# The second MLP layer of 256-token chunks as a seven-product block product, with its sums on GpSimd

## The chip, the cores and the metric

The kernel runs on one core of a Trainium2 chip. The metric is device microseconds (us) of one execution. A core has five engines, each of which executes its own queue of instructions in the order of the program: TensorE (PE in the profile; PEld is its loading of stationary operands), VectorE (DVE), ScalarE (ACT), GpSimd (POOL) and SyncE (SP, which here issues all the DMAs). They wait for one another on semaphores.

## The reference, cut to what matters

```python
# q, k, v: (8, 8, 576, 64) float32; w_in: (512, 2048), w_out: (2048, 512)
scores = scale * q @ k.T                       # 64 heads of 576 x 576
kth    = 32nd largest of each row
attn   = softmax of the row, with all below kth masked out
x      = (attn @ v)  laid out as 4608 tokens x 512
h      = x @ w_in
g      = max(0.01 * h, h)
out    = g @ w_out                             # 4608 x 512
```

The weights come as 64-bit floats; the kernel turns them to float32 itself, at the start.

## The kernel before, in words

**Attention.** Work is cut into 144 units, 18 for each of the 8 batches. A unit is 128 rows of queries for one pair of heads: two score matrices of 128 x 576. Of the 18, 16 are 128 query rows of one pair ("whole"), and 2 are the 64 left-over rows of two pairs ("left"). A unit goes through these stages:

- `scores`: q·k on PE into PSUM (L235), for two units at a time, and four copies by ACT into `s_sb` (L242).
- `top_k` on DVE: one pairwise max and min of the halves of each row (L306, two instructions), then four rounds of MAX8 (L311) and MATCH_REPLACE8 (L314). The 32nd value ends up in `tops`.
- `limits` on POOL: three tiny instructions (L324, L325, L326) that make `nleast` and `nbias` of `tops`.
- `mask` (L330) and `exponents` (L333) on ACT, two of each, and `sums` (L338), which makes `ze`.
- `reciprocals` on DVE (L342: `rz` of `ze`), and `normalize` on POOL (L345, two instructions of 128 x 576).
- `transpose`: two copies by ACT that split the 32-bit weights into 16-bit halves (L354), two DMAs to DRAM (L355), and one transposing DMA back to `wT` (L359).
- `values`: `wT` times v on PE (L398, L410), for two units at a time, and copies by ACT to `x` (L422).

**The MLP.** The tokens are taken in 19 chunks, two of 128 and 17 of 256. For a chunk of 256, the first layer makes 8 pieces `ph` (two blocks of 128 of the 2048 hidden columns each, L467: matmuls with 256 moving columns, four deep), and ACT writes each through leaky ReLU to `gT` (L473). The second layer then makes, for each 128 tokens, one `pz` of 512 columns, 16 matmuls deep (L479), which ACT copies to `o_sb` (L488), and SP sends out (L489). A float32 matmul shows as two MATMUL records in the profile, each with its LDWEIGHTS.

**The order** is written out by hand. The main loop runs over steps s, one unit each. In step s, DVE does `top_k` of unit s. Within the step these go to the queues in this order: `limits(s-1)` and `normalize(s-2)` early, then on ACT `mask(s-1)`, the first of `exponents(s-1)`, the two splits of s-2, the second of `exponents(s-1)`, `sums(s-1)`. At the end of each even step come `values` of two units (s-4 and s-3 from unit 14 on), their copies to `x`, and the `scores` of units s+2 and s+3 with their four copies. Between these parts there are seven places a step (`mlp_steps`), at which the MLP generator of the running chunk is advanced piece by piece; the budget of a place is the work of the chunk divided by the places left until the next chunk's tokens are ready. The last place of a step lies after the scores. What a piece gives to ACT, POOL and SP stands in their queues at the same place.

The rows of chunk 17 are ready 8 units before the end, those of chunk 18 with the last unit; what is left is done after the last step.

**Scores kept in DRAM.** For the 12 units 26, 27, 34, 35, 62, 63, 70, 71, 98, 99, 106, 107, the scores are made in the first steps (`keep_scores`, L286 on PE, L290 on ACT), stored in DRAM and fetched when due (`fetch_scores`); `load_early` brings their q and k into buffers named `raw`, three of which hold the raw weights at the start. Later those buffers serve as three more pairs of q and k buffers, besides five.

The second layer as it stands in the code:

```python
for r0 in range(0, n, P):
    pz = ps_ml.tile([P, 512], F32, name="pz", tag="ml")
    for f in range(NFC):
        nc.tensor.matmul(pz[0:m, 0:DMODEL], gT[:, f, r0:r0 + m], w_out[f // 4][:, f % 4, :], ...)
```

Of the kernel before, what the change touches and what calls it, by code (L numbers as in the profile page):

```python
# [20 lines left out]
def kernel(  # L21
# [23 lines left out]
    HP = DMODEL // P  # L45
# [20 lines left out]
    kept = ctx.enter_context(tc.tile_pool(name="kept", bufs=1, space=bass.MemoryType.DRAM))  # L66
# [93 lines left out]
    qk_of, v_of = {}, {}  # L160

    def load_qk(pi, at_once=True):
        if pi % (LOADED + 3) < LOADED:
            qt = loads.tile([P, S], F32, name="qt")
            kt = loads.tile([P, S], F32, name="kt")
        else:
            raw = raws.tile([P, WCH, 4], U16, name="raw").rearrange("p n w -> p (n w)").bitcast(F32)
            qt, kt = raw[:, 0:S], raw[:, S:2 * S]
# [75 lines left out]
    def first_scores(u):  # L244
# [10 lines left out]
        u.s = [u.both[:, i, :] for i in range(2)]  # L255
        for i in range(2):
            nc.scalar.copy(u.s[i].rearrange("p (h n) -> p h n", h=2), ps[i][:, :, 0:HS])  # L257

    early_of = {}

    def load_early(us):

        raw = raws.tile([P, WCH, 4], U16, name="raw").rearrange("p n w -> p (n w)").bitcast(F32)
        at = 0
        for pi in sorted({u.pairs[0] for u in us}):
            kt = raw[:, at:at + S]
            nc.sync.dma_start(kt, kT[pi])
            at += S
            for u in us:
                if u.pairs[0] == pi:  # L270
                    early_of[u] = raw[:, at:at + P], kt
                    nc.sync.dma_start(early_of[u][0], qT[pi][:, u.q0:u.q0 + P])
                    at += P

    kept_of = {}

    def keep_scores(u):

        k = len(kept_of)
        qt, kt = early_of.pop(u)  # L280
        ps = [ps_sc.tile([P, 2, 512], F32, name="wide", bufs=2) if (2 * k + i) % 3 else
              ps_sc.tile([P, 2, 512], F32, name="narrow") for i in range(2)]
        for half in range(2):
            for i, _, side, _ in u.parts:
                d = slice(side * D, (side + 1) * D)
                nc.tensor.matmul(ps[i][:, half, 0:HS], qt[d, :], kt[d, half * HS:(half + 1) * HS],  # L286
                                 start=True, stop=True)
        both = gT.rearrange("p f n -> p (f n)")[:, k % 3 * 2 * S:(k % 3 + 1) * 2 * S]
        for i in range(2):
            nc.scalar.copy(both[:, i * S:(i + 1) * S].rearrange("p (h n) -> p h n", h=2), ps[i][:, :, 0:HS])  # L290
        kept_of[u] = kept.tile([P, 2 * S], F32, name=f"kept{k}")
        nc.sync.dma_start(kept_of[u], both)

    def fetch_scores(u):
        u.both = work.tile([P, 2, S], F32, name="s_sb", bufs=5)
        u.s = [u.both[:, i, :] for i in range(2)]
        nc.sync.dma_start(u.both.rearrange("p i n -> p (i n)"), kept_of[u])

    def top_k(u):

# [147 lines left out]
    def turned(j, g_of):  # L448
# [3 lines left out]
        nc.scalar.copy(gT[:, 4 * j:4 * (j + 1), 0:P], pt)  # L452
        yield 2 * P

    def mlp(ch):

        n = CHUNKS[ch]
        t0 = sum(CHUNKS[:ch])
        x = x_of[ch]
        if ch < EARLY:  # L460
            yield from hidden_of_few(ch, x)
        for f0 in range(0, NFC if ch >= EARLY else 0, 2):
            ph = ps_ml.tile([P, 2, CHMAX], F32, name="ph", tag="ml")
            for i in range(2):
                f = f0 + i
                for c in range(HP):
                    nc.tensor.matmul(  # L467
                        ph[:, i, 0:n], w_in[c][:, f * P:(f + 1) * P], x[c][:, 0:n],
                        start=(c == 0), stop=(c == HP - 1),
                    )  # L470
                    if c == 1 or i == 0 and c == HP - 1:
                        yield 2 * max(n, 225)
            nc.scalar.activation(gT[:, f0:f0 + 2, 0:n], ph[:, :, 0:n], AF.Prelu, alpha=SLOPE)  # L473
            yield 2 * max(n, 225)
        for r0 in range(0, n, P):
            m = min(P, n - r0)
            pz = ps_ml.tile([P, 512], F32, name="pz", tag="ml")
            for f in range(NFC):
                nc.tensor.matmul(  # L479
                    pz[0:m, 0:DMODEL], gT[:, f, r0:r0 + m], w_out[f // 4][:, f % 4, :],  # L480
                    start=(f == 0), stop=(f == NFC - 1),
                )
# [4 lines left out]
            o_sb = work.tile([P, DMODEL], F32, name="o_sb", bufs=1)  # L487
            nc.scalar.copy(o_sb[0:m], pz[0:m, 0:DMODEL])  # L488
            nc.sync.dma_start(out[t0 + r0:t0 + r0 + m, :], o_sb[0:m])  # L489
# [40 lines left out]

    steps = units

    KEPT = (26, 62, 98)
    EARLY_SCORES = {0: 4, 1: 2, 2: 1, 3: 2, 4: 1, 5: 2}

    def unit(n):
        return steps[n] if 0 <= n < len(steps) else None

# [25 lines left out]
    with tc.manual_schedule():  # L564
        last = {p: n for n, u in enumerate(steps) for p in u.pairs}
        starts = {p: n for n, u in reversed(list(enumerate(steps))) for p in u.pairs}

        to_keep = [[steps[n] for n in (a, a + 1, a + 8, a + 9)] for a in KEPT]
        early_units = {u for us in to_keep for u in us}
        to_load, to_keep = list(to_keep), [u for us in to_keep for u in us]  # L570
        assert all(len(u.pairs) == 1 for u in to_keep)

        def score_early(count):

            for _ in range(min(count, len(to_keep))):
                keep_scores(to_keep.pop(0))
                if len(to_keep) % 4 == 0 and to_load:
                    load_early(to_load.pop(0))

        def load_more(s):  # L580

            at_once = 2
# [13 lines left out]
                    break  # L596
            while len(qk_of) < NPAIR:
                n = len(qk_of)
                if n < LOADED or not to_keep and n < LOADED + 3:
                    load_qk(n)  # L600
                elif not to_keep and last[n - LOADED - 3] + 8 <= s and not waiting:
                    load_qk(n, at_once=False)
                else:
                    break

# [4 lines left out]
        for n in range(len(jobs) + 1):  # L610
# [11 lines left out]
                    pass  # L622
            if n:
                load_weights(n + 2)
            if n >= len(jobs) - 2 and to_load:
                load_early(to_load.pop(0))
            if 0 <= n - len(jobs) + HP + 1 < HP:
                load_qk(n - len(jobs) + HP + 1)

# [18 lines left out]
        def keep(weighed, *place):  # L648
            for u, po in weighed:
                keep_values(u.pairs[0], po, u.b, u.q0)  # L650
            attended(*place)

        for s in range(len(steps) + LAG + 1):
            assert s < 7 or not to_keep
            cur, old, older, new = unit(s), unit(s - 1), unit(s - 2), ()
            if s % 2 == 0:
                new = [u for u in steps[s + 2:s + 4] if u]
# [33 lines left out]
                keep_transposed(older) if s - 2 in HASTY else transpose(older, lambda: mlp_steps(budget))  # L691
            if not older or s - 2 in HASTY:
                mlp_steps(budget)
            if unit(s + 3) in early_units:
                fetch_scores(unit(s + 3))
            else:
                load_waiting()
            slot()
            slot()
            mlp_steps(budget)  # L700
# [3 lines left out]
            mlp_steps(budget)  # L704
            if not at_once:
                keep(weighed, s, MIDDLE)
            if new and new[0] in early_units:
                new = ()
# [69 lines left out]
```

## Time and profile before

| what | value |
|---|---|
| median of 3 runs | 1460.23 us (1459.14 to 1461.59) |
| the profiled execution's own time | 1464.25 us |
| its span, first to last instruction | 1462.5 us |
| PE busy | 1399.0 us, 96% of the span |
| DVE busy | 1313.9 us, 90% |
| ACT busy | 1103.2 us, 75% |
| POOL busy | 738.5 us, 50% |
| mean granted clock of PE | 0.986 |
| first and last start of `top_k` (L306) | 61.32 us, 1366.41 us |

A row of a group reads: line, engine, operation, output<-input, shapes, how many; then busy time of the group in us, mean of one in ns; then the idle time of the engine just before these instructions, and what ended it. Matmuls are pipelined, so that busy time divided by the number of records is nearer to the cost of one than its mean duration is: 482.6 us / 2176 = 222 ns for a record with 256 moving columns (L467), 505.7 us / 1152 = 439 ns for one with 512 (L479).

### The profile page before, as it was taken

To read this page: it belongs to the slowest core of one execution; us is meant where nothing else is said; L and a number is where in the kernel's file an instruction comes from. 1 tells how busy PE (TensorE), PEld (TensorE's weight loads), DVE (VectorE), ACT (ScalarE), POOL (GpSimd) and SP (SyncE) were. 2 spreads that over 40 slices of the span, in tenths; PEclk is the share of its full clock that TensorE was granted. 3 is DMA by queue.
4 is the path that set the end of the run, shared out by engine and by line. 5 is a ranking of instruction groups with operands and counts; after the bars stand their busy time and mean duration, and the time that the engine had idled before them with its cause. 6 is when DMAs were issued, how large, how long until landed. Compare 5 with 4: busy or idle time off the path is not lost.

```text
span 1462.5 us, 25892 instructions
## 1 busy us (share of the span) xinstructions
PE 1399.0 (96%) x8980; PEld 904.8 (62%) x8980; DVE 1313.9 (90%) x3401; ACT 1103.2 (75%) x1984; POOL 738.5 (50%) x744
## 2 busy tenths in 40 slices
PE   7847989999999999999999999999999999999998
PEld 2324547575666666666666666666666666666674
DVE  7998999999999999999999999999999999999500
ACT  8878877777787787777787878778778787778710
POOL 3245555555555555555555555555555555555500
PEclk9968999999999999999999999999999999999999
DMA  8967542657456555666655755666656665545610
GB/s 329 336 215 214 145 122 89 188 148 174 143 155 189 157 151 145 177 181 176 184 156 157 183 143 147 169 188 175 186 158 169 165 158 142 156 126 136 148 46 14
DMA packets 394995, 239.13 MB, mean 164 GB/s; under 512 B 334576, under 2 KB 336112, under 8 KB 392944
## 3 DMA queue, kind: packets, MB, share of 16 engines
q1 hardware_dynamic: 394864, 237.48, 57.8%
q8 instruction: 70, 1.15, 0.4%
q14 instruction: 61, 0.50, 0.1%
HBM read 55.77 MB, written 99.09 MB: 106 GB/s over the span
## 4 chain that ended last, share of the span: by engine, by line
PE 73%; DVE 13%; ACT 5%; DMA 5%; POOL 2%; issue 1%; SPq 0%; DVEq 0%; ACTq 0%; POOLq 0%
PE ph L467 27%; PE pz L479 27%; PE wide L398 9%; DVE tops L311 5%; PE wide L235 4%; DVE pairs L314 4%; PE narrow L235 3%; DMA wT<-apart 2%; ACT split L354 2%; POOL s_sb L345 1%; DVE pairs L306 1%; DMA apart<-split 1%; PE wide L410 1%; PE ph L435 1%; ACT s_sb L333 1%
## 5 line engine op out<-in xcount | busy, mean ns | idle before, releaser
L345 POOL TENSOR_SCALAR s_sb<-s_sb,rz 128x576 f32<-128x576 f32 x288 | 497.1, 1735 | 290.7 <-DVE rz L342 289.2
L311 DVE MAX8 tops<-pairs 128x8 f32<-128x288 f32 (+1 forms) x1152 | 637.7, 594 | 0.0
L479 PE MATMUL pz<-w_out,gT 128*128 128x512 f32 x1152 | 505.7, 595 | 0.5 <-ACT scale L440 0.5
L467 PE MATMUL ph<-x,w_in 128*128 128x256 f32 x2176 | 482.6, 381 | 0.0
L314 DVE MATCH_REPLACE8 pairs<-tops,pairs 128x288 f32<-128x288 f32 (+1 forms) x864 | 461.4, 541 | 0.0
L467 PEld LDWEIGHTS ph<-x,w_in 128*128 128x128 f32 x2176 | 409.5, 190 | 77.7 <-issue 23.5
L479 PEld LDWEIGHTS pz<-w_out,gT 128*128 128x128 f32 x1152 | 217.0, 190 | 265.4 <-issue 262.8
L354 ACT COPY split<-s_sb 128x1152 uint16<-128x1152 uint16 x280 | 310.4, 1149 | 83.8 <-POOL s_sb L345 82.4
L324 POOL TENSOR_SCALAR nleast<-tops 128x2 f32<-128x2 f32 x144 | 74.7, 519 | 308.3 <-DVE tops L311 308.3
L333 ACT ACTIVATE s_sb<-s_sb,nbias 128x576 f32<-128x576 f32 x288 | 222.2, 771 | 0.0
L306 DVE TENSOR_TENSOR pairs<-s_sb 128x576 f32<-128x576 f32 x288 | 206.9, 758 | 9.5
L330 ACT ACTIVATE s_sb<-s_sb,nleast 128x576 f32<-128x576 f32 x288 | 207.2, 772 | 1.6 <-POOL nleast L324 1.6
L398 PE MATMUL wide<-wT,vt 128*64 128x128 f32 (+1 forms) x2560 | 160.3, 282 | 15.1 <-DMA wT<-apart 10.0
L398 PEld LDWEIGHTS wide<-wT,vt 128*64 128x64 f32 (+1 forms) x2560 | 131.7, 137 | 64.8 <-issue 34.3
L473 ACT ACTIVATE gT<-ph 128x512 f32<-128x512 f32 x136 | 80.7, 593 | 60.3 <-PE ph L467 60.1
L422 ACT COPY x<-wide 128x128 f32<-128x128 f32 (+1 forms) x160 | 32.2, 260 | 108.3 <-PE wide L398 94.4
L242 ACT COPY s_sb<-wide 128x704 f32<-128x704 f32 x130 | 98.1, 755 | 8.9 <-PE wide L235 2.9
L325 POOL TENSOR_TENSOR nbias<-tops 128x2 f32<-128x2 f32 x144 | 95.2, 661 | 0.0
L235 PE MATMUL wide<-kt,qt 64*64 64x352 f32 x704 | 73.0, 477 | 1.0 <-ACT s_sb L257 0.7
L488 ACT COPY o_sb<-pz 128x512 f32<-128x512 f32 x36 | 21.0, 584 | 65.0 <-PE pz L479 65.0
L342 DVE RECIPROCAL rz<-ze 128x2 f32<-128x2 f32 x144 | 22.7, 158 | 48.8 <-ACT ze L338 48.5
L314 DVE MATCH_VALUE_LOAD pairs<-tops,pairs 128x8 f32 x864 | 65.0, 75 | 0.0
(70 smaller groups left out, 783.9 us busy)
## 6 DMA issues: line engine op xcount, KB each, us to landing
apart<-split SPq DMA_DIRECT2D x280, 288.0 KB, 2.1
raw<-in_weights_dram SPq DMA_DIRECT2D x15, 1024.0 KB, 7.2
vt<-in_vk_dram SPq DMA_DIRECT2D x32, 320.0 KB, 3.5
out_dram<-o_sb SPq DMA_DIRECT2D x36, 256.0 KB, 3.5
kept<-gT SPq DMA_DIRECT2D x12, 576.0 KB, 3.6
s_sb<-kept SPq DMA_DIRECT2D x12, 576.0 KB, 4.7
qt<-in_qT_dram SPq DMA_DIRECT2D x20, 288.0 KB, 3.3
kt<-in_kT_dram SPq DMA_DIRECT2D x20, 288.0 KB, 3.5
```

Of the source, the lines that this page charges most:

```text
L235: nc.tensor.matmul(to[r0:r0 + LEFT, i, :], qt[d, q0:q0 + LEFT], kt[d, k0:k1], start=True, stop=True)
L242: nc.scalar.copy(u.both[:, :, k0:k1], to)
L306: nc.vector.tensor_tensor(pairs[:, :, n, :], u.both[:, :, 0:HS], u.both[:, :, HS:S], op)
L311: nc.vector.max(out=u.tops[:, i, r, :], in_=rest[i])
L314: nc.vector.match_replace(out=rest[i], in_to_replace=u.tops[:, i, r, :], in_values=rest[i], imm_value=LOWEST)
L330: nc.scalar.activation(u.s[i], u.s[i], AF.Prelu, bias=u.nleast[:, i:i + 1], scale=1.0, alpha=BELOW)
L333: nc.scalar.activation(u.s[i], u.s[i], AF.Exp, bias=u.nbias[:, i:i + 1], scale=SCALE, accum_out=u.z[:, i:i + 1])
L345: nc.gpsimd.tensor_scalar(u.s[i], u.s[i], u.rz[:, i:i + 1], None, ALU.mult)
L354: nc.scalar.copy(split, pairs[:, :, h])
L398: nc.tensor.matmul(po[n * D:(n + 1) * D, side, 0:P], v_of[u.pairs[0]][k, at, side, :], u.wT[k, at + side * NKC if at + 1 < NKC else at, :] ...
L467: nc.tensor.matmul(ph[:, i, 0:n], w_in[c][:, f * P:(f + 1) * P], x[c][:, 0:n], start=(c == 0), stop=(c == HP - 1),)
L479: nc.tensor.matmul(pz[0:m, 0:DMODEL], gT[:, f, r0:r0 + m], w_out[f // 4][:, f % 4, :], start=(f == 0), stop=(f == NFC - 1),)
```

## The change

The second layer of a 256-token chunk is taken as a product of two-by-two blocks. `gT` is cut into tokens 0 to 127 and 128 to 255 (rows) by hidden columns 0 to 1023 and 1024 to 2047 (columns): g11, g12, g21, g22. `w_out` is cut into hidden halves by output halves of 256 columns. Instead of eight block products there are seven (Strassen's form in Winograd's arrangement), each 8 matmuls deep with 256 moving columns. Three of the sums that the form asks for are made in PSUM by going on adding to `px` without clearing it; the others are made by POOL:

- once, in steps 0 to 5, the weight sums t1, t2, t4 (six instructions of 128 x 1024 elements, `sum_weights`), into the three `raw` buffers; and two of the same size that overwrite a block of `w_out` before the first 256-token chunk (`sum_last_weights`);
- in each chunk, after the fourth and the eighth leaky ReLU, three instructions of 128 x 512: s1, s2, and g21 in place; later one of 128 x 1024 (g12 in place) and three of 128 x 256 on the partial outputs.

ACT makes seven copies of 128 x 256 out of PSUM for each chunk, instead of two of 128 x 512, and SP sends four pieces out instead of two. A piece `ph` now takes blocks f0 and f0 + 8, so that one activation writes both halves.

The `raw` buffers being taken, no scores are kept in DRAM: all units' scores are made by `scores`. There are seven pairs of q and k buffers in place of five and three. In batches 2, 4 and 6 the two left units stand before the last four whole ones, not after them. The DMA scratch area is made smaller, which frees SBUF.

```diff
-    LOADED, LOADED_V = 5, 5
+    LOADED, LOADED_V = 7, 5
...
-        units += left + whole if first else whole + left
+        if first:
+            units += left + whole
+        elif b:
+            units += whole[:-HP] + left + whole[-HP:]
+        else:
+            units += whole + left
...
-    early_of = {}
-    def load_early(us):
...
-    def keep_scores(u):
...
-    def fetch_scores(u):
...
+    HALF, COLS = NFC // 2, DMODEL // 2
+    def sum_weights():
...
+        for g in range(2):
+            t1, t2, t4 = [summed[name][:, 4 * g:4 * (g + 1), :] for name in ("t1", "t2", "t4")]
+            nc.gpsimd.tensor_tensor(t1, w_block(0, 1, g), w_block(0, 0, g), ALU.subtract)
+            yield
+            nc.gpsimd.tensor_tensor(t2, w_block(1, 1, g), t1, ALU.subtract)
+            yield
+            nc.gpsimd.tensor_tensor(t4, w_block(1, 0, g), t2, ALU.subtract)
+            yield
+    def sum_last_weights():
+        for g in range(2):
+            nc.gpsimd.tensor_tensor(w_block(0, 1, g), w_block(1, 1, g), w_block(0, 1, g), ALU.subtract)
...
+        if ch < EARLY:
+            yield from plain(ch, n, t0, x)
+            return
+        if ch == EARLY:
+            sum_last_weights()
+        halves_of_g = gT.rearrange("p (h f) n -> p h f n", h=2)
+        (g11, g21), (g12, g22) = [[halves_of_g[:, h, :, r * P:(r + 1) * P] for r in range(2)] for h in range(2)]
...
+        for f0 in range(HALF):
+            ph = ps_ml.tile([P, 2, CHMAX], F32, name="ph", tag="ml")
...
+            nc.scalar.activation(halves_of_g[:, :, f0, :], ph, AF.Prelu, alpha=SLOPE)
+            if f0 % 4 == 3:
+                at = slice(f0 - 3, f0 + 1)
+                nc.gpsimd.tensor_tensor(s1[:, at, :], g21[:, at, :], g22[:, at, :], ALU.add)
+                nc.gpsimd.tensor_tensor(s2[:, at, :], s1[:, at, :], g11[:, at, :], ALU.subtract)
+                nc.gpsimd.tensor_tensor(g21[:, at, :], g11[:, at, :], g21[:, at, :], ALU.subtract)
+            yield 2 * n
+        def product(to, g, w, first=False):
+            for f in range(HALF):
+                nc.tensor.matmul(to, g[:, f, :], w(f), start=(first and f == 0), stop=(f == HALF - 1),
+                                 skip_group_check=not first)
+                if f % 4 == 3:
+                    yield 4 * COLS
+        def keep_sum(ps):
+            part = work.tile([P, COLS], F32, name="o_sb", bufs=6)
+            nc.scalar.copy(part, ps)
+            return part
...
+        px, py, pz = pa[:, 0:COLS], pb[:, 0:COLS], pb[:, COLS:2 * COLS]
+        yield from product(px, g11, lambda f: w_at(f, 0), first=True)
+        p1 = keep_sum(px)
+        yield from product(py, g12, lambda f: w_at(f + HALF, 0), first=True)
+        p2 = keep_sum(py)
+        yield from product(px, s2, of("t2"))
+        u2 = keep_sum(px)
+        add(p1, p2)
+        nc.gpsimd.tensor_tensor(g12, g12, s2, ALU.subtract)
+        yield from product(pz, s1, of("t1"), first=True)
+        p5 = keep_sum(pz)
+        put(p1, 0, 0)
+        yield from product(px, g21, lambda f: w_at(f, 1))
+        u3 = keep_sum(px)
+        yield from product(pz, g12, lambda f: w_at(f + HALF, 1))
+        p35 = keep_sum(pz)
+        add(u3, p5)
+        yield from product(px, g22, of("t4"))
+        c21 = keep_sum(px)
+        add(u2, p35)
+        put(u3, 1, 1)
+        put(c21, 1, 0)
+        put(u2, 0, 1)
...
-        return NFC * HP * max(n, 225) + -(-n // P) * NFC * DMODEL
+        return NFC * HP * n + 7 * HALF * COLS
...
-            if unit(s + 3) in early_units:
-                fetch_scores(unit(s + 3))
-            else:
-                load_waiting()
+            load_waiting()
...
-            score_early(EARLY_SCORES.get(s, 0))
             budget = slot_budget(s + 1)
             mlp_steps(budget)
             load_more(s)
+            next(weight_sums, None)
```

More of the change, by code (lines that the diff above doesn't have):

```diff
@@ L65 @@
     halves = ctx.enter_context(tc.tile_pool(name="halves", bufs=3, space=bass.MemoryType.DRAM))
-    kept = ctx.enter_context(tc.tile_pool(name="kept", bufs=1, space=bass.MemoryType.DRAM))
     ps_sc = ctx.enter_context(tc.tile_pool(name="ps_sc", bufs=1, space=bass.MemoryType.PSUM))
@@ L162, in load_qk @@
     def load_qk(pi, at_once=True):
-        if pi % (LOADED + 3) < LOADED:
-            qt = loads.tile([P, S], F32, name="qt")
-            kt = loads.tile([P, S], F32, name="kt")
-        else:
-            raw = raws.tile([P, WCH, 4], U16, name="raw").rearrange("p n w -> p (n w)").bitcast(F32)
-            qt, kt = raw[:, 0:S], raw[:, S:2 * S]
+        qt = loads.tile([P, S], F32, name="qt")
+        kt = loads.tile([P, S], F32, name="kt")
         waiting.extend([(qt, qT[pi]), (kt, kT[pi])])
@@ L257, in first_scores @@
             nc.scalar.copy(u.s[i].rearrange("p (h n) -> p h n", h=2), ps[i][:, :, 0:HS])
-    early_of = {}
-    def load_early(us):
[L263 to L275, printed above, removed]
-    def keep_scores(u):
[L279 to L292, printed above, removed]
-    def fetch_scores(u):
-        u.both = work.tile([P, 2, S], F32, name="s_sb", bufs=5)
-        u.s = [u.both[:, i, :] for i in range(2)]
-        nc.sync.dma_start(u.both.rearrange("p i n -> p (i n)"), kept_of[u])
     def top_k(u):
@@ L453, in turned, with w_at, w_block @@
         yield 2 * P
+    HALF, COLS = NFC // 2, DMODEL // 2
+    summed = {}
+    def w_at(f, j):
+        return w_out[f // 4][:, f % 4, j * COLS:(j + 1) * COLS]
+    def w_block(i, j, g):
+        return w_out[2 * i + g][:, :, j * COLS:(j + 1) * COLS]
+    def sum_weights():
+        for name in ("t1", "t2", "t4"):
+            t = raws.tile([P, WCH, 4], U16, name="raw").rearrange("p n w -> p (n w)").bitcast(F32)
+            summed[name] = t.rearrange("p (f n) -> p f n", n=COLS)
+        for g in range(2):
[9 more added lines that the diff above has]
+            nc.gpsimd.tensor_tensor(w_block(0, 1, g), w_block(1, 1, g), w_block(0, 1, g), ALU.subtract)
     def mlp(ch):
@@ L459, in mlp @@
         x = x_of[ch]
+        if ch < EARLY:
[5 more added lines that the diff above has]
+        (g11, g21), (g12, g22) = [[halves_of_g[:, h, :, r * P:(r + 1) * P] for r in range(2)] for h in range(2)]
+        s1 = raws.tile([P, HALF, P], F32, name="top", bufs=2)
+        s2 = raws.tile([P, HALF, P], F32, name="top", bufs=2)
+        for f0 in range(HALF):
+            ph = ps_ml.tile([P, 2, CHMAX], F32, name="ph", tag="ml")
+            for i in range(2):
+                f = f0 + i * HALF
+                for c in range(HP):
+                    nc.tensor.matmul(
+                        ph[:, i, 0:n], w_in[c][:, f * P:(f + 1) * P], x[c][:, 0:n],
+                        start=(c == 0), stop=(c == HP - 1),
+                    )
+                    if c == 1 or i == 0 and c == HP - 1:
+                        yield 2 * n
[5 more added lines that the diff above has]
+                nc.gpsimd.tensor_tensor(g21[:, at, :], g11[:, at, :], g21[:, at, :], ALU.subtract)
+            yield 2 * n
@@ new lines, in product, with add @@
+        def product(to, g, w, first=False):
[8 more added lines that the diff above has]
+            return part
+        def add(part, other):
+            nc.gpsimd.tensor_tensor(part, part, other, ALU.add)
@@ new lines, in put, with of @@
+        def put(part, r, j):
+            nc.sync.dma_start(out[t0 + r * P:t0 + (r + 1) * P, j * COLS:(j + 1) * COLS], part)
+        def of(name):
+            return lambda f: summed[name][:, f, :]
+        pa = ps_ml.tile([P, 512], F32, name="pz", tag="ml")
+        pb = ps_ml.tile([P, 512], F32, name="pz", tag="ml")
+        px, py, pz = pa[:, 0:COLS], pb[:, 0:COLS], pb[:, COLS:2 * COLS]
+        yield from product(px, g11, lambda f: w_at(f, 0), first=True)
+        p1 = keep_sum(px)
+        yield from product(py, g12, lambda f: w_at(f + HALF, 0), first=True)
@@ L460, in mlp, with plain @@
+        c21 = keep_sum(px)
[3 more added lines that the diff above has]
+        put(u2, 0, 1)
+        yield 0
+    def plain(ch, n, t0, x):
         if ch < EARLY:
@@ L486, in mlp @@
                     yield from turned(NFC // 4 - 1, few[ch])
-            o_sb = work.tile([P, DMODEL], F32, name="o_sb", bufs=1)
-            nc.scalar.copy(o_sb[0:m], pz[0:m, 0:DMODEL])
-            nc.sync.dma_start(out[t0 + r0:t0 + r0 + m, :], o_sb[0:m])
+            for j in range(2):
+                o_sb = work.tile([P, COLS], F32, name="o_sb", bufs=6)
+                nc.scalar.copy(o_sb, pz[:, j * COLS:(j + 1) * COLS])
+                nc.sync.dma_start(out[t0 + r0:t0 + r0 + m, j * COLS:(j + 1) * COLS], o_sb)
             yield 2 * DMODEL
@@ L531 @@
     steps = units
-    KEPT = (26, 62, 98)
-    EARLY_SCORES = {0: 4, 1: 2, 2: 1, 3: 2, 4: 1, 5: 2}
     def unit(n):
@@ L566 @@
         starts = {p: n for n, u in reversed(list(enumerate(steps))) for p in u.pairs}
[L568 to L578, printed above, removed]
         def load_more(s):
@@ L598, in load_more @@
                 n = len(qk_of)
-                if n < LOADED or not to_keep and n < LOADED + 3:
+                if n < LOADED:
                     load_qk(n)
-                elif not to_keep and last[n - LOADED - 3] + 8 <= s and not waiting:
-                    load_qk(n, at_once=False)
+                elif last[n - LOADED] // 2 * 2 - 1 <= s and (not waiting or starts[n] <= s + 5):
+                    load_qk(n, at_once=starts[n] <= s + 5)
                 else:
@@ L624 @@
                 load_weights(n + 2)
-            if n >= len(jobs) - 2 and to_load:
-                load_early(to_load.pop(0))
             if 0 <= n - len(jobs) + HP + 1 < HP:
@@ L651, in keep @@
             attended(*place)
+        weight_sums = sum_weights()
         for s in range(len(steps) + LAG + 1):
-            assert s < 7 or not to_keep
             cur, old, older, new = unit(s), unit(s - 1), unit(s - 2), ()
@@ L693 @@
                 mlp_steps(budget)
-            if unit(s + 3) in early_units:
-                fetch_scores(unit(s + 3))
-            else:
-                load_waiting()
+            load_waiting()
             slot()
@@ L706 @@
                 keep(weighed, s, MIDDLE)
-            if new and new[0] in early_units:
-                new = ()
             if new and s < HURRY:
@@ L764 @@
     }
-    nc = _bacc.Bacc("TRN2", target_bir_lowering=False, num_devices=1)
+    nc = _bacc.Bacc("TRN2", target_bir_lowering=False, num_devices=1,
+                     dynamic_dma_scratch_size=1024)
     arrays, args = {}, []
```

## The prediction

> **What bounds the kernel now.** I read the page first, then the waits, then VectorE's instructions in order of time, then one stretch of the steady state with all engines, then the chain that ended last.
>
> The page's shares and its costliest groups:
>
> ```profile
> PE 1399.0 (96%) x8980; PEld 904.8 (62%) x8980; DVE 1313.9 (90%) x3401; ACT 1103.2 (75%) x1984; POOL 738.5 (50%) x744
> ...
> L345 POOL TENSOR_SCALAR s_sb<-s_sb,rz 128x576 f32<-128x576 f32 x288 | 497.1, 1735 | 290.7 <-DVE rz L342 289.2
> ...
> L479 PE MATMUL pz<-w_out,gT 128*128 128x512 f32 x1152 | 505.7, 595 | 0.5 <-ACT scale L440 0.5
> L467 PE MATMUL ph<-x,w_in 128*128 128x256 f32 x2176 | 482.6, 381 | 0.0
> ```
>
> PE looks like the bound, with 96%. But the starts of `top_k` on DVE (first, two neighbours, last) say otherwise:
>
> ```profile
> 61.32 1.41 DVE L306 TENSOR_TENSOR pairs<-s_sb 128x576 f32<-128x576 f32 x2
> ...
> 706.75 1.43 DVE L306 TENSOR_TENSOR pairs<-s_sb 128x576 f32<-128x576 f32 x2
> 715.60 1.45 DVE L306 TENSOR_TENSOR pairs<-s_sb 128x576 f32<-128x576 f32 x2
> ...
> 1366.41 1.43 DVE L306 TENSOR_TENSOR pairs<-s_sb 128x576 f32<-128x576 f32 x2
> ```
>
> A step in which DVE never waits takes 8.77 to 8.85 us, mean 8.815. From 61.32 to 1366.41 there are 143 steps: 1305.1 us, of which 143 x 8.815 = 1260.5 is DVE's own pace. The excess is 44.6 us, and the list of waits says what it is:
>
> ```profile
> ACT split L354 <- POOL s_sb L345: 82.4, 52, 5.8
> ...
> DVE rz L342 <- ACT ze L338: 48.5, 45, 6.9
> ```
>
> (The 6.9 us one lies behind the last step.) So DVE sets the pace, and loses 3.4% to `ze` coming late from ACT. Why it comes late is seen at the end of an even step; the rows are start, duration, engine:
>
> ```profile
> 706.81 0.79 POOL L324 TENSOR_SCALAR nleast<-tops 128x2 f32<-128x2 f32 x1 [2.21 <-DVE tops L311]
> ...
> 709.93 3.44 POOL L345 TENSOR_SCALAR s_sb<-s_sb,rz 128x576 f32<-128x576 f32 x2 [1.38 <-DVE rz L342]
> ...
> 711.84 0.60 ACT L473 ACTIVATE gT<-ph 128x512 f32<-128x512 f32 x1
> ...
> 712.33 1.43 ACT L330 ACTIVATE s_sb<-s_sb,nleast 128x576 f32<-128x576 f32 x2
> ...
> 714.42 2.19 ACT L354 COPY split<-s_sb 128x1152 uint16<-128x1152 uint16 x2
> ...
> 716.52 0.77 ACT L333 ACTIVATE s_sb<-s_sb,nbias 128x576 f32<-128x576 f32 x1
> ...
> 717.41 0.20 ACT L338 ACTIVATE ze<-z 128x2 f32<-128x2 f32 x1
> ...
> 718.55 0.15 DVE L342 RECIPROCAL rz<-ze 128x2 f32<-128x2 f32 x1
> ```
>
> POOL does `limits` the moment `tops` is there (706.8) and `normalize` the moment `rz` is there (709.9); ACT comes to the masks only at 712.3, after the copies of values and scores and a leaky ReLU. `ze` is there at 717.6, DVE takes it at 718.55: 0.94 us of slack. The whole loop (rz, normalize, split, DMA, transpose, values, copies, mask, exponents, ze, rz three steps later) is as long as DVE's three steps. It is a loop of latencies; a faster PE shortens it only where PE is late.
>
> **The change part by part.** All against the profiled execution's span, 1462.5 us (own time 1464.25, so 1.75 around it, and 4.0 above the median of 1460.23).
>
> *PE.* Per 256-token chunk the second layer goes from 64 records of 439 ns (28.1 us) to 7 x 8 x 2 = 112 of 222 ns (24.9 us): -3.2 us, 17 times, -55 us. The 12 units' early scores (L286, 34.6 us) go too, from a stretch (before 115 us) in which PE waits anyway: 0. Their scores return to the steady state: L235's four groups are 175.3 us for 65 pairs of units, 2.7 each, six pairs, +16 us. Net some -39 us in the steady state. DVE sets the pace, so its worth is the DVE waits that come from a late PE, at most the 44.6 us. I take 40: with less PE work and the new stalls below, PE will hardly be late any more.
>
> *The end.* The chain that ended last is PE alone:
>
> ```profile
> 1387.18 13.93 PE pz L479 x32
> ...
> 1403.38 27.82 PE ph L467 x128
> 1431.21 27.48 PE pz L479 x64
> ```
>
> The last chunk's second layer shortens by 3.2 us, and the last values, now behind 13.93 us of chunk 17, come earlier: the rz before them was at 1384.1, and rz to values takes about 14 us elsewhere, so 1398.4 instead of 1401.1, with a part of the 6.9 us wait for the last `ze` on top. Bounds -3.2 and -12; I take -7.
>
> *ACT, SP.* ACT gets seven copies of 128x256 for two of 128x512: between L422's 128x128 (0.27 us) and L488's 128x512 (0.58), so about 0.37, +1.4 us a chunk; and 6 x 2.6 us for the scores' copies. ACT idles 264 of the 1251 us between 115 and 1366, in waits: cost 0 by that cover, up to 40 without it. Each copy is queued one piece after its product, so it seldom waits. SP sends 36 pieces more and issues 42 transfers of kept scores and their q and k fewer. Each output transfer waits for POOL or ACT with the splits' DMAs behind it, but is queued a product or more after its sum: 0, bound +5.
>
> *POOL, by amount.* Per chunk six sums of 512, one of 1024, three of 256 elements per partition. No two-input sum of that size is in the trace. Nearest row: L345, 1735 ns for 576 elements with one input, so 1.54 us for 512. Lower end 0.57 (the 16-bit copy L131, 1135 ns for 1024), upper end 3.08 (twice L345, for two inputs). At 1.54 it is 14.6 us per chunk, 249 us in all, of 724 idle: by amount it fits.
>
> *POOL, by order: the step that decides.* Everything that the MLP gives POOL stands behind `normalize` of its step and ahead of `limits` of the next. Three sums (s1, s2, g21) are queued right after the fourth and eighth leaky ReLU of a chunk and wait for it. In the changed program's order, the fourth stands in eleven of 17 chunks on ACT after the scores' copies of an even step, immediately ahead of the masks, just as at 711.84 above. There POOL, which now does `limits` at 706.8, must first wait for the leaky ReLU and do three sums. ACT's masks wait for `nleast`, and `normalize` comes behind that. In numbers, from the stretch above: leaky ReLU done 712.44; three sums 4.62, 717.06; `limits` as long as now (706.81 to 708.55, 1.74), 718.8; `normalize` 3.44, 722.24; two splits 2.19, 724.43; second exponents 0.89 (716.52 to 717.41), 725.32; `ze` 725.5. DVE wants it at 718.55: a stall of 6.9 us on the engine that sets the pace, where there is none now. Eleven times: +76 us. At the lower end of the sum's price the stall is 4.0 (+44), at the upper 11.6 (+127).
>
> Three more groups stand at the end of an odd step, where ACT's masks follow too (about 4 us each by the same count, as `rz` comes later there), and three at other unlucky places (about 2 each): +18. The other 17 follow the masks and end before `limits` is wanted: 0, up to 1 each. The weight sums in steps 0 to 5: three microseconds of POOL a step where L345 and `limits` fill 5 of 8.8: 0, up to 5.
>
> The Trainium skill ("GPSIMD Engine Reference", 3.1) gives 4497 ns for a two-input float32 add of 2048 elements, which would make 1.12 us of 512 (an estimate by that page), stalls of 5.6 us, and a total some 14 us lower. Its section 4.1 says to put elementwise adds on VectorE; here that engine has no time left.
>
> *Sum.* 1462.5 - 40 - 7 + 76 + 18 = 1509.5 span, 1511 with what lies around it, 1507 in the terms of the median.
>
> **The rivals.**
>
> *The bursts are hidden (faster).* ACT reaches the fourth leaky ReLU earlier against DVE once PE is light, so that POOL's sums fall into the 2.2 us that it idles before `tops`. For it: POOL is idle half the time, and PE's lateness is part of why ACT is late. Against it: in the stretch above PE was not late, it waited 0.35 us for `wT` in its values. With nothing left of the stalls, 1462.5 - 44.6 - 7 = 1411, the least that DVE allows, 1409 by the median; with 1.5 us left of each burst and a fifth of the rest, +20, 1430. It decides once a burst costs less than half of the 6.9 (47 of gain against 94 of stalls).
>
> *POOL and DVE hold each other up (slower still).* One `normalize` overlaps the two-input L306 (217.01, 1.41 us):
>
> ```profile
> 217.19 4.44 POOL L345 TENSOR_SCALAR s_sb<-s_sb,rz 128x576 f32<-128x576 f32 x2 [3.74 <-DVE rz L342]
> ```
>
> It took 4.44 us where the others take 3.44; L306 lost nothing. Which of them loses when POOL is first, no row shows. If it is DVE, each g12 sum (2.7 to 3.1 us, put behind `normalize`, so running when the next L306 is due) costs up to 1.3 us, 17 times, +22: 1529. The skill ("SBUF — State Buffer", "SBUF: two separate sides") calls the shared port an exclusive lock that whoever is first keeps for the instruction, which speaks for this rival; by it the sum would be those 22 us higher.
>
> *It comes out even.* Stalls of about 3.4 us each cancel the gain, within 0.2% (some 3 us, about what a measurement of this kernel can tell from no change).
>
> **How the numbers follow.** The order of the queues is certain, and even the lowest price of a sum leaves 44 + 10 of stalls against 47: forecast 0.63. Hidden bursts 0.24, contention on top 0.10, even 0.03. Slower 0.73, same 0.03, faster 0.24. The forecast's own range is 1470 (lower price) to 1545. The range that should hold 8 in 10 takes in the slower half of the faster rival: 1428 to 1545.
>
> **What would show it.** Right: DVE's wait for `ze` grows from 48 to over 100 us, with stalls of 5 to 8 us every eight steps; `nleast` waits for ACT's leaky ReLU behind the sums instead of for `tops`, ACT's masks wait for `nleast` (1.6 us now); the second layer's records cost 222 ns; PE's share falls below 92%. Wrong: steps stay at 8.82 us, or L306 grows, or the sums of 512 take well under 0.6 us.

## The result, and the profile after

The changed kernel takes 1501.71 us (median of 4 runs, 1500.08 to 1503.06) against 1459.68 for the kernel before: ratio 1.0287, 95% interval 1.027 to 1.0305. The forecast was 1507, slower: the time came within 6 us and the sign was right. The cause that the forecast's largest term names is not the cause.

The page of the changed kernel, its shares and the groups that answer to those shown before. In a group's row the last two parts are busy us and mean ns, then the idle time ahead and what ended it.

```profile
span 1501.3 us, 28007 instructions
...
PE 1364.0 (91%) x9892; PEld 1068.3 (71%) x9892; DVE 1375.6 (92%) x3401; ACT 1109.1 (74%) x2071; POOL 955.8 (64%) x922
...
L271 DVE MAX8 tops<-pairs 128x8 f32<-128x288 f32 (+1 forms) x1152 | 636.3, 592 | 0.0
...
L266 DVE TENSOR_TENSOR pairs<-s_sb 128x576 f32<-128x576 f32 x288 | 269.6, 975 | 10.3 <-ACT split L314 0.5
L477 PE MATMUL pz<-w_out,gT 128*128 128x256 f32 x1088 | 243.2, 381 | 0.0
```

PE did get lighter: a record of the second layer costs 243.2 / 1088 = 224 ns, as forecast, and PE's share fell from 96% to 91%. DVE got heavier, by 62 us, without a single instruction more, and all of it is in one line: the pairwise max and min (L306 before, L266 now), from a mean of 758 ns to 975. MAX8 stayed as it was. In the list of waits, the one that the forecast rests on became smaller, not larger (48.5 us before, 31.5 now). ACT's masks, as forecast, wait more for `nleast` than the 1.6 us before (in all, times, longest):

```profile
ACT s_sb L290 <- POOL nleast L284: 35.0, 18, 5.6
...
DVE rz L302 <- ACT ze L298: 31.5, 18, 7.7
```

Where the time went, in the two profiled executions, from the first and the last start of `top_k`:

```profile
62.47 1.42 DVE L266 TENSOR_TENSOR pairs<-s_sb 128x576 f32<-128x576 f32 x2
...
1410.62 1.43 DVE L266 TENSOR_TENSOR pairs<-s_sb 128x576 f32<-128x576 f32 x2
```

Between them lie now 1348.15 us instead of 1305.09; DVE's own pace for these 143 steps is 1260.5. The excess was 44.6 us; the waits for `ze` ahead of the last one were 41.6 (all but 2.0 of them in these steps). The excess is 87.6 now, with 23.8 of such waits (all but 1.3 in these steps) and 62.4 for the longer L266. What follows the last start fell from 96.1 to 90.7 us; the first start moved by 1.2. Sum: 1462.5 + 43.1 - 5.4 + 1.2 = 1501.4.

One stretch shows how L266 grows: an instruction in each row, in order of time.

```profile
640.03 1.43 DVE L266 TENSOR_TENSOR pairs<-s_sb 128x576 f32<-128x576 f32 x2
...
640.84 0.67 POOL L285 TENSOR_TENSOR nbias<-tops 128x2 f32<-128x2 f32 x1
...
643.21 3.45 POOL L305 TENSOR_SCALAR s_sb<-s_sb,rz 128x576 f32<-128x576 f32 x2 [1.38 <-DVE rz L302]
...
644.80 0.60 ACT L467 ACTIVATE gT<-ph 128x512 f32<-128x512 f32 x1 [0.71 <-PE ph L461]
...
646.62 1.28 POOL L470 TENSOR_TENSOR top<-gT 128x512 f32<-128x512 f32 x1
...
647.97 1.27 POOL L471 TENSOR_TENSOR top<-top,gT 128x512 f32<-128x512 f32 x1
...
648.88 2.73 DVE L266 TENSOR_TENSOR pairs<-s_sb 128x576 f32<-128x576 f32 x2
...
649.21 1.78 POOL L472 TENSOR_TENSOR gT<-gT 128x512 f32<-128x512 f32 x1
```

The unit at 640.03 finds POOL free of sums: 1.43 us for the two instructions. The unit at 648.88 starts while the sum L471 runs, and L472 starts before its second instruction: 2.73 us. L472 pays too, 1.78 us instead of 1.28. Over all 144 units, 48 have a sum of POOL's running beside L266; these 48 lose 62.4 us, the other 96 lose nothing (below 0.03 us each). By what runs beside: s2 with g21, 24 units, 1.41 us each; s1 with what follows it, 4 units, 1.5; g12, 12 units, 0.72; g12 after an output sum, 3 units, 2.2; weight sums, 5 units, 1.0 to 1.6.

The same stretch shows what the prediction had wrong: the sums wait for the leaky ReLU at 644.80, and `limits` (L285) and `normalize` (L305) stand ahead of them on POOL, not behind them.

### The profile page after: what moved, and what is told of

Same layout as the page of the kernel before. It is cut to its first block, busy times and chain, and to the rows that moved or that the text cites. A ratio compares the mean times of both kernels' runs of the same rounds, so it can differ in the third digit from the quotient of the medians.

```text
span 1501.3 us, 28007 instructions
## 1 busy us (share of the span) xinstructions
PE 1364.0 (91%) x9892; PEld 1068.3 (71%) x9892; DVE 1375.6 (92%) x3401; ACT 1109.1 (74%) x2071; POOL 955.8 (64%) x922
## 3 DMA queue, kind: packets, MB, share of 16 engines
q8 instruction: 78, 1.28, 0.3%
## 4 chain that ended last, share of the span: by engine, by line
DVE 55%; PE 21%; issue 6%; ACT 6%; POOL 5%; DMA 5%; DVEq 0%; SPq 0%; ACTq 0%; POOLq 0%
DVE tops L271 26%; DVE pairs L274 20%; PE pz L477 8%; DVE pairs L266 7%; PE ph L461 6%; POOL s_sb L305 4%; DMA wT<-apart 4%; PE wide L358 3%; ACT split L314 3%; PE wide L235 1%; ACT s_sb L293 1%; PE ph L395 1%; DMA apart<-split 1%; DMA raw<-in_weights_dram 1%; PE narrow L235 1%
## 5 line engine op out<-in xcount | busy, mean ns | idle before, releaser
L305 POOL TENSOR_SCALAR s_sb<-s_sb,rz 128x576 f32<-128x576 f32 x288 | 497.7, 1737 | 240.7 <-DVE rz L302 240.7
L266 DVE TENSOR_TENSOR pairs<-s_sb 128x576 f32<-128x576 f32 x288 | 269.6, 975 | 10.3 <-ACT split L314 0.5
L477 PE MATMUL pz<-w_out,gT 128*128 128x256 f32 x1088 | 243.2, 381 | 0.0
L358 PE MATMUL wide<-wT,vt 128*64 128x128 f32 (+1 forms) x2560 | 181.6, 294 | 63.7 <-DMA wT<-apart 35.7
L477 PEld LDWEIGHTS pz<-w_out,gT 128*128 128x128 f32 x1088 | 207.3, 191 | 31.6 <-issue 4.3
L358 PEld LDWEIGHTS wide<-wT,vt 128*64 128x64 f32 (+1 forms) x2560 | 144.6, 144 | 109.0 <-DMA wT<-apart 46.3
L235 PE MATMUL wide<-kt,qt 64*64 64x352 f32 x1136 | 116.4, 482 | 44.4 <-ACT s_sb L242 25.1
L477 PE MATMUL pz<-raw,top 128*128 128x256 f32 x544 | 124.2, 383 | 1.5 <-ACT o_sb L484 1.2
L477 PEld LDWEIGHTS pz<-raw,top 128*128 128x128 f32 x544 | 102.2, 190 | 22.6 <-issue 6.6
L235 PEld LDWEIGHTS wide<-kt,qt 64*64 64x64 f32 x1136 | 37.9, 138 | 64.7 <-ACT x L382 28.4
L285 POOL TENSOR_TENSOR nbias<-tops 128x2 f32<-128x2 f32 x144 | 77.7, 540 | 0.0
L470 POOL TENSOR_TENSOR top<-gT 128x512 f32<-128x512 f32 x34 | 43.9, 1290 | 51.3 <-ACT gT L467 51.2
```

The source lines that it names most:

```text
L235: nc.tensor.matmul(to[r0:r0 + LEFT, i, :], qt[d, q0:q0 + LEFT], kt[d, k0:k1], start=True, stop=True)
L266: nc.vector.tensor_tensor(pairs[:, :, n, :], u.both[:, :, 0:HS], u.both[:, :, HS:S], op)
L305: nc.gpsimd.tensor_scalar(u.s[i], u.s[i], u.rz[:, i:i + 1], None, ALU.mult)
L358: nc.tensor.matmul(po[n * D:(n + 1) * D, side, 0:P], v_of[u.pairs[0]][k, at, side, :], u.wT[k, at + side * NKC if at + 1 < NKC else at, :] ...
L477: nc.tensor.matmul(to, g[:, f, :], w(f), start=(first and f == 0), stop=(f == HALF - 1), skip_group_check=not first)
```

## The experiments

Theory P: a GpSimd sum and VectorE's two-input instruction hold each other up; the loss is the 62 us of L266. Theory Q, on record in the prediction: sums ahead of `limits` and `normalize` in GpSimd's queue make the masks, and through them `ze`, late.

The diffs are shortened to what matters.

**1. The sums left out.** s1 and s2 are names for g21 and g22, and the other sums of the chunks are gone, so that the output is not the MLP's.

```diff
-        s1 = raws.tile([P, HALF, P], F32, name="top", bufs=2)
-        s2 = raws.tile([P, HALF, P], F32, name="top", bufs=2)
+        s1, s2 = g21, g22
...
-                nc.gpsimd.tensor_tensor(s1[:, at, :], g21[:, at, :], g22[:, at, :], ALU.add)
-                nc.gpsimd.tensor_tensor(s2[:, at, :], s1[:, at, :], g11[:, at, :], ALU.subtract)
-                nc.gpsimd.tensor_tensor(g21[:, at, :], g11[:, at, :], g21[:, at, :], ALU.subtract)
...
-            nc.gpsimd.tensor_tensor(part, part, other, ALU.add)
+            pass
...
-        nc.gpsimd.tensor_tensor(g12, g12, s2, ALU.subtract)
```

> The changed kernel without the ten sums that GpSimd makes for each 256-token chunk (s1 and s2 are replaced by g21 and g22 as they stand, so the output is not that of the MLP); the six weight sums of the first steps and the two later ones stay, and so does everything on PE, ACT and SP. Theory P (port): the loss lies in L266, VectorE's two-input instruction, which went from 758 to 975 ns in the mean (62 us in all) because a GpSimd sum holds the port that both use; without the sums its mean is below 780 ns and the time falls by 62 us plus most of the 24 us of waits for ze, to 1415 to 1440. Theory Q (queue, the step that the prediction rests on): the loss comes of sums ahead of limits and normalize in GpSimd's queue, through late masks and a late ze; then the 24 us of waits for ze go, L266 stays near 975 ns, and the time is about 1478.

Measured: 1458.1 us, 0.996 of the kernel before (0.9945 to 0.9976), 43 us below the changed kernel, or 48 by the two ratios (the kernel before took 1464.0 beside this run).

```profile
L266 DVE TENSOR_TENSOR pairs<-s_sb 128x576 f32<-128x576 f32 x288 | 214.3, 784 | 10.8 <-ACT s_sb L242 0.7 <-ACT split L314 0.5
```

L266 is back, but for some 7 us that the weight sums of the first steps and one of the two later ones still cost. The waits for `ze` did not go: 31.6 us ahead of the last one, more than with the sums. So P holds for L266, Q does not; but the time stays 18 us above the upper end of what P's account expected. The likely reason is that DVE, held up by the sums, had been covering waits for `ze` that now show; run 3 shows such covering. That left a second question: why a lighter PE does not remove them (runs 9 and 10).

**2. The sums put into GpSimd's idle stretches.** All sums are made, in smaller parts, from a list that is emptied behind `limits` and behind `normalize`.

```diff
+    def in_gap(limit):
+        while due and due[0][0] <= limit:
...
+    GAPS = (75, 205)
...
                 limits(old)
...
+                in_gap(GAPS[0])
...
                 weights_of(older)
+            in_gap(GAPS[1])
             mlp_steps(budget)
```

The limits are in units of 10 ns.

> All of the changed kernel's sums, cut smaller (s1 and s2 per two blocks, g21 and g12 in two parts of 128x512, the last weight sums in four) and put off: at most one of 128x256 directly behind limits, and at most about 2.05 us of them directly behind normalize, in which GpSimd idles 2.2 us before VectorE starts its next unit; the six weight sums go behind limits of the first steps. Theory P: as many elements are added, but hardly any beside L266, whose mean falls to 760 to 820 ns; 1420 to 1450, faster than both kernels. Theory Q: as much work stands in GpSimd's queue between the steps of the attention, and 30 us or more of waits for ze remain; 1480 to 1505.

Measured: 1544.7 us, ratio 1.0552 (1.0535 to 1.057): a miss, above both expectations. L266 is nearly back (808 ns), so P's part came true, but the waits for `ze` grew. The first row is from the list of waits, the others show how they come about in one chunk:

```profile
DVE rz L302 <- ACT ze L298: 114.8, 51, 6.9
...
532.75 5.34 PE L502 MATMUL pz<-w_out,gT 128*128 128x256 f32 x16 [5.47 <-POOL gT L442]
...
538.13 0.37 ACT L509 COPY o_sb<-pz 128x256 f32<-128x256 f32 x1 [5.49 <-PE pz L502]
...
540.58 0.17 DVE L302 RECIPROCAL rz<-ze 128x2 f32<-128x2 f32 x1 [3.27 <-ACT ze L298]
```

The sum g12 (`gT` L442) had been put off until PE needed it. PE waits 5.47 us for it; ACT's copy of the product stands ahead of the second split and the second exponents in ACT's queue and waits with it, and `ze` is 3.27 us late. What PE does behind the product (values and scores) is late too, and so is the next step's `ze`. Ten chunks show such a pair of steps, 70 us of the 107.9 of waits ahead of the last one; PE waited 65.6 us in all for sums that write `gT`. So the sums made `ze` late, as Q has it, but by way of PE and ACT's queue and not of late masks.

A sum put between `limits` and `normalize` whose leaky ReLU was not done yet held POOL up as well, 13 times in the steps, for 1.4 to 6.9 us. Most of that time passed before `rz` was there: in ten of the 13, `normalize` started 1.3 us after `rz` (0.1 is usual). The next `ze` was at most 0.4 us late, the one after it 0 to 3.0.

**3, 4, 5. The port by itself.** The kernel before with one idle GpSimd operation behind `normalize` in each step, into a tile that nobody reads, for which the DMA scratch area is made smaller. Nothing of the MLP changes.

```diff
             normalize(u, 0)
             normalize(u, 1)
+            nc.gpsimd.tensor_tensor(spare[:, 0:1536], w_in[0][:, 0:1536], w_in[1][:, 0:1536], ALU.add)
```

The second run has 768 in place of 1536, the third `tensor_scalar(spare[:, 0:1152], w_in[0][:, 0:1152], 2.0, None, ALU.mult)`.

> The kernel before, with one two-input GpSimd sum of 128x1536 of weights into a tile that nobody reads, directly behind normalize in each step; nothing waits for it but GpSimd's own queue. At 2.3 ns per element (the 2430 ns of L506 for 1024) it takes 3.6 us, from 6.7 to 10.2 us of a step, and so reaches 1.4 us into the next unit's two-input instruction (due at 8.8). Theory P: that instruction's pair grows by 1.2 to 1.5 us in each of 140 steps and the time by 130 to 190 us, to 1590 to 1650. Theory Q: limits comes 1.4 us late, which the masks have in hand (ACT reaches them 5.6 us later at the end of even steps): L306 stays at 758 ns and the time within 1460 to 1490.

> As the run before, with 768 elements in place of 1536: 1.8 us, from 6.7 to 8.5 us of a step, over before the next two-input instruction of VectorE is due. Theory P: that instruction stays below 780 ns and the time within 1455 to 1475. Theory Q: much the same, 1460 to 1475; what tells the two apart is the difference between this run and the long one.

> As the long idle sum in the kernel before, but an operation with one input (a product with a constant) of 128x1152, which at L345's 3.0 ns per element runs as long, 3.5 us, from 6.7 to 10.2 us of a step. If it is any GpSimd instruction that reads, which holds VectorE's two-input instruction up: L306's pair grows by 1.2 to 1.5 us in each step as with the two-input sum, 1590 to 1610. If only GpSimd's two-input instructions do: L306 stays at 758 ns, 1460 to 1490.

Measured: 1596.0, 1475.9 and 1521.0 us, where the kernel before took 1464.0 beside the first two and 1463.7 beside the third. One stretch of each, the long sum first, then the short one, then the operation with one input:

```profile
705.03 3.48 POOL L635 TENSOR_TENSOR spare<-w_in,w_in 128x1536 f32<-128x1536 f32 x1
...
707.21 2.58 DVE L307 TENSOR_TENSOR pairs<-s_sb 128x576 f32<-128x576 f32 x2
```

```profile
705.41 1.83 POOL L635 TENSOR_TENSOR spare<-w_in,w_in 128x768 f32<-128x768 f32 x1
707.60 1.43 DVE L307 TENSOR_TENSOR pairs<-s_sb 128x576 f32<-128x576 f32 x2
```

```profile
703.42 3.13 POOL L635 TENSOR_SCALAR spare<-w_in 128x1152 f32<-128x1152 f32 x1
...
705.67 1.92 DVE L307 TENSOR_TENSOR pairs<-s_sb 128x576 f32<-128x576 f32 x2
```

The long sum runs 1.30 us into L307 (705.03 + 3.48 - 707.21) and L307 loses 1.15; over 139 units 1.27 each, 176 us. The time grew by 132 only, since the waits for `ze` fell from 48.5 to 9.6 us: a DVE that is held up covers them. The short sum is over before L307 is due and costs it nothing; what the kernel loses (12 us) is 16 units in the first steps, where `normalize` stands later and the sum does reach L307, at 1.02 us each. This is P shown by itself: the same queue, the same kind of work, and what decides is whether it reaches L307. The operation with one input lies between the two answers expected: beside 0.88 us of it (703.42 + 3.13 - 705.67) L307 loses 0.49, in the mean 0.70 a unit. That is not a share of the overlap: in the first steps, where it runs 2.52 us into L307, L307 loses 2.13. In all 139 units the loss is the overlap less 0.39 us, and in the long sum's 139 the overlap less 0.15.

**6. The queue that the prediction had assumed.** The first MLP place of a step moved ahead of `limits` and `normalize`.

```diff
             slot()
+            mlp_steps(budget)
             if old:
                 limits(old)
...
                 weights_of(older)
-            mlp_steps(budget)
             if old:
                 mask(old, 0)
```

> The changed kernel with the first of the seven MLP places of a step moved ahead of limits and normalize, behind VectorE's first part; nothing else. ACT's order is the same, but the sums behind a leaky ReLU of that place now stand ahead of limits in GpSimd's queue, which is the queue that the prediction took the changed kernel to have. If the prediction's price holds (6.9 us a chunk, sums behind a leaky ReLU at 5.7 us of a step, then limits, normalize, splits, exponents), VectorE's waits for ze grow from 24 to 90 us or more, and the time to 1560 to 1600. If the loop has more in hand than was counted, the waits stay below 50 us and the time below 1530.

Measured: 1582.0 us, waits for `ze` 112.8 us. The stretch that the prediction had described, met here:

```profile
584.59 0.60 ACT L467 ACTIVATE gT<-ph 128x512 f32<-128x512 f32 x1 [0.89 <-PE ph L461]
585.27 1.27 POOL L470 TENSOR_TENSOR top<-gT 128x512 f32<-128x512 f32 x1 [8.62 <-ACT gT L467]
...
590.36 1.44 ACT L290 ACTIVATE s_sb<-s_sb,nleast 128x576 f32<-128x576 f32 x2 [5.17 <-POOL nleast L284]
...
597.75 0.20 ACT L298 ACTIVATE ze<-z 128x2 f32<-128x2 f32 x1
...
597.99 0.17 DVE L302 RECIPROCAL rz<-ze 128x2 f32<-128x2 f32 x1 [6.17 <-ACT ze L298]
```

POOL idles 8.62 us for the leaky ReLU, the masks wait 5.17 us, and from the leaky ReLU's end to `ze` it takes 12.8 us (585.19 to 597.95), where the prediction had worked out 13.1. Twelve chunks show a wait for `ze` of 6.0 to 8.6 us each, where 6.9 had been worked out. The price was right; the changed kernel just does not have this order.

**7. The idle stretches again**, with no sum there whose input may still be in the making (a sum is taken behind `limits` only two steps after it is queued, behind `normalize` one step after), with g12 and g21 queued earlier and a chunk's last s1 and s2 made at once, and with the units' order of the kernel before.

```diff
-    def in_gap(limit):
-        while due and due[0][0] <= limit:
+    def in_gap(limit, age):
+        while due and due[0][0] <= limit and now[0] >= due[0][3] + age:
...
-        elif b:
-            units += whole[:-HP] + left + whole[-HP:]
...
+        units += left + whole if first else whole + left
```

> The sums in GpSimd's idle stretches again, but no sum there whose input is still being made: behind limits only sums queued two steps earlier (up to 1.3 us of them), behind normalize those queued a step earlier (up to 2.05 us); the last s1 and s2 of a chunk at once; g21 and g12 queued earlier. Also the units' order of the kernel before. If the 115 us of waits for ze in the first try came of sums that stood ahead of normalize and waited for a leaky ReLU, they fall below 40 us; L266 has a mean below 800 ns; 1440 to 1465. If the sums cost by their amount wherever they stand: 1490 or more.

Measured: 1451.8 us, 0.9922 of the kernel before (0.9891 to 0.9953), 50 us below the changed kernel (53 by the ratios): all of the change's arithmetic, and 0.8% faster than the kernel before.

```profile
L261 DVE TENSOR_TENSOR pairs<-s_sb 128x576 f32<-128x576 f32 x288 | 214.9, 786 | 10.3 <-DVE tops L266 0.5 <-ACT s_sb L237 0.2
```

It makes as many elements of sums as the changed kernel (POOL is busy 973.1 us). The cleanest comparison is run 8, which has the same units' order and was measured beside the same runs of the kernel before: 1493.4 us. The 41.6 us between them come of where the sums stand, how they are cut, and when the outputs are sent. PE's waits for sums that write `gT` fell to 0.2 us, and of the seven waits of sums for a leaky ReLU that are left, four lie behind the last step; which of the edits did what was not tried.

**8. The units' order alone**, put back in the changed kernel.

```diff
-        elif b:
-            units += whole[:-HP] + left + whole[-HP:]
...
+        units += left + whole if first else whole + left
```

> The changed kernel with the order of units of the kernel before (left units behind all the whole ones in batches 2, 4 and 6): one part of the change undone. In the changed kernel, chunk 11 is ready at unit 89 and chunk 12 at 95, six units later, where all other chunks have eight; steps 93 to 103 exceed VectorE's own pace by some 12 us there, and by 10 us in the run without sums. If the short interval is the cause (53 us of MLP budgeted into six steps), 8 to 14 us go: 1488 to 1494. If not: 1499 to 1504.

Measured: 1493.4 us, ratio to the kernel before 1.0203 (1.0177 to 1.023), against 1.0287 for the changed kernel: some 8 to 12 us of its loss are the new order's. It leaves chunk 11 only six units, which is the likely reason and as much as had been expected of it.

**9, 10. What a lighter PE is worth.** Run 9 is run 1 with the order of run 8. Run 10 also cuts each product to four matmuls of eight.

```diff
-            for f in range(HALF):
+            for f in range(HALF // 2):
```

> The changed kernel without the chunks' sums (as in the first run, so its output is not that of the MLP) and with the units' order of the kernel before: what the lighter second layer alone is worth. The first run kept 31.6 us of waits for ze ahead of the last one, 11 of them in steps 96 to 102. If these came of the six-unit interval, 20 to 24 us are left and the time is 1446 to 1452; if not, it stays at 1455 to 1460.

> As the run before, with each of the seven products cut to four matmuls of eight (half of the second layer left out, and the planner told so): 12.4 us less of PE per chunk, 211 us in all. Theory L (loop): the waits for ze that are left come of the loop of latencies from rz over DMA, values, copies and exponents to the next ze, which a lighter PE does not shorten: 12 us or more of them remain ahead of the last one. Theory T (throughput): they come of a late PE: below 6 us remain. Either way the last chunk's second layer shortens by 12.4 us at the end, so that the time is 1420 to 1440.

Measured: 1451.1 and 1455.3 us, with the kernel before at 1456.4 beside them (one run each). Run 9 against run 1 does not settle the order's worth: the ratio to the kernel before is 0.996 in both, the waits for `ze` ahead of the last one are 25.1 us instead of 31.6. The waits of run 10:

```profile
PE wide L353 <- DMA wT<-apart: 118.9, 48, 5.3
...
DVE rz L297 <- ACT ze L293: 50.2, 31, 7.4
```

With PE busy 1199 us instead of 1344, the waits for `ze` grew from 32.0 to 50.2 us, PE now waits for `wT`, and the time rose by 4 (single runs). What the end gained (90.0 to 78.6 us behind the last start) the waits took back. So theory T is out: with a lighter PE the waits do not go. Theory L is what is left, but it gives no reason for their growth, and the time expected for run 10, which had them no longer than before, was missed. Why they grew with half the work was not tried further; PE's granted clock was lower too, 0.942 against 0.976 in run 9.

## Why the prediction was right or wrong, point by point

**DVE sets the pace: right.** In the changed kernel a step without a disturbance still takes 8.8 us (640.03 to 648.88), and taking 144 us from PE (run 10 against run 9) gains nothing.

**The cost of the new records on PE: right** (224 ns against 222).

**"I take 40" of the 44.6 us that go with a late PE: mis-sized.** The waits fell by 17.8 us in the changed kernel (41.6 to 23.8). In run 9 25.1 are left ahead of the last one, in run 10 43. The prediction had itself called the waits a loop of latencies, and then credited most of them to PE's lateness.

**The end, -7: right in kind**, -5.4 measured.

**ACT and SP at nothing:** nothing in the profile speaks against it; ACT's busy time grew by 6 us.

**The price of a sum, 1.54 us for 512 elements by L345: too high.** Measured 1.28 (L470). The Trainium skill ("GPSIMD Engine Reference", 3.1) had led to an estimate of 1.12; the truth lies between, nearer to it.

**"POOL, by order: the step that decides", +76 and +18: the step that failed.** It took the leaky ReLU just ahead of the masks for the last place of the even step. It is in the first place of the next one, which on ACT also stands between the scores' copies and the masks, but on POOL behind `limits` and `normalize` of that step. Each engine's order was read by itself, and ACT's order does not tell the two places apart. Of the stalls, few came: 18 waits for `ze` in all. At three of the 34 groups the sums, ahead of the next `limits`, wait 3.8 to 5.0 us for a leaky ReLU (to 252.16, 436.52 and 875.04); the four waits for `ze` that follow add up to 8.7 us, where +94 was forecast. Behind the masks' other waits for `nleast`, 1.0 to 1.5 us each between the first steps and the last, no wait for `ze` follows in the next step. Run 6 shows that the stalls would have come, at the price given.

**The rival "POOL and DVE hold each other up": the cause**, given 0.10 and +22 us. It was sized for the g12 sums alone; the s1, s2, g21 groups were counted as stalls, or as ending before `limits` is wanted. Behind `normalize`, three sums from about 6.6 us of a step reach past 8.8, where the next unit starts: 62.4 us, nearly three times the 22. The Trainium skill ("SBUF — State Buffer", "SBUF: two separate sides") calls the shared port an exclusive lock for whoever is first. For two-input sums and for the product with a constant the runs agree but for a constant (the overlap less 0.15 and less 0.39 us). `normalize`, which has one input and a factor per partition, shows no such lock when it is first; the measurement decides here:

```profile
879.54 3.45 POOL L305 TENSOR_SCALAR s_sb<-s_sb,rz 128x576 f32<-128x576 f32 x2
...
881.84 1.43 DVE L266 TENSOR_TENSOR pairs<-s_sb 128x576 f32<-128x576 f32 x2
```

They run side by side for 1.1 us, and neither takes longer. That answers, for `normalize`, what the prediction said that no row shows. Why it differs was not tried.

**Why the time came out all the same.** From the forecast's span of 1509.5: -94 for stalls that were not there, +62.4 for L266, +22.2 for waits that stayed, +1.6 at the end: 1501.7, where the profiled span is 1501.3 (the median of 1501.71 is alike by chance). Two errors of opposite sign; a time that is met proves no mechanism.

## What to carry to other kernels

When an idle engine is to take work over, look not only at how much idle time it has but at which instruction of the bounding engine runs beside each stretch of it: here the same GpSimd sums made the kernel 2.0% slower than before where some ran beside VectorE's two-input instruction (run 8) and, in smaller parts in GpSimd's idle stretches, 0.8% faster (run 7, the same order of units). And for an in-order queue, work out the position of a new instruction on every engine from the loop that emits it; the same place in the program lies ahead of an instruction on one engine and behind it on another.

## What the runs showed of the hardware that was not expected

- A GpSimd operation holds VectorE's two-input instruction up for the rest of its own time, less a constant: 0.15 us for a two-input sum (runs 3 and 4), 0.39 us for a product with a constant (run 5), from 0.9 to 2.8 us of overlap. `normalize`, a product with a value per partition, held it up in none of seven units of the changed kernel and runs 6 and 8, beside 0.6 to 1.1 us.
- Per element the one-input operations were not the faster: 3.13 us for 1152 by a constant (2.7 ns each) and 1.74 for 576 by a value per partition (3.0), against 3.46 for 1536 (2.3) with two inputs.
- MAX8 and MATCH_REPLACE8 on VectorE did not suffer beside GpSimd's sums: 592 ns for MAX8 in the changed kernel, 594 in the one before; 539 and 541 for MATCH_REPLACE8.
